# Another warm-up, another order of the first transfers, and new ranks for a planned attention and feed-forward kernel

## Chip, core and metric

The kernel runs on one core of a Trainium2 chip. The metric is the device time of one execution in microseconds, here the median of three runs. Lower is better.

## What is computed

Three parts follow each other: a gated linear attention (4 batches, 8 heads, 768 tokens, head size 32, state size 16), a channel mix with 256 to 1,024 to 256 channels and a sigmoid gate, and a second feed-forward layer with 256 to 2,048 to 256 channels. All of it is computed on 3,072 tokens, in float32.

```python
log_a = np.log(np.clip(a, 1e-06, 1.0))
for c in range(nc):                       # chunks of the sequence
    cum = np.cumsum(la, axis=-1)
    L = np.exp(cum[:, :, :, None] - cum[:, :, None, :]) * causal
    y_intra = (C B^T * L) x
    y_inter = (C state) * exp(cum)
    state = exp(sum(la)) * state + sum(B x * exp(cum[-1] - cum))
xk = mu_k * x + (1 - mu_k) * x_prev;  xr likewise with mu_r
k = relu(xk @ w_k);  v = (k * k) @ w_v;  r = sigmoid(xr @ w_r);  x = r * v
h = x @ w_in;  g = h - tanh(h);  out = g @ w_out
```

## The kernel before

**Tiles.** The tokens are cut into 12 groups of 256 for attention (four chunks of 64) and 6 blocks of 512 for the two feed-forward layers. Every large product is done in three parts (high with high, low weights with high, high with low) on values split into a high and a low half; a block of the channel mix is 4 units, one of the second layer 8 units (`up2`, the polynomial `poly_a` to `poly_c`, `g_high`, `g_low`, `down2`).

**Weights.** They arrive as 64-bit numbers in blocks of 512 KB (`raw`, two buffers), 9 for the channel mix and 16 for the second layer, and each is decoded: `square` on ScalarE, then `top`, `sign`, `bottom`, `guard` on VectorE, `high` on either of the two, `low` on VectorE (lines 322 to 365). `NW` (line 34) says how many of the nine are fetched in the prologue; the others are fetched by the plan when a raw buffer is free. An x block or a bc block of attention has 384 KB.

**Prologue.** `START` (lines 60 to 64) is an order written out by hand; each name is a step in `fns` (lines 711 to 728), and what a step issues on an engine stands in that engine's queue in this order. `qz` clears the tile `quiet`; `wa`, `ws`, `wb` multiply it with itself (`fill`, `small`); their results are not used. `Da`, `Dla`, `Dca` load the decays, `Db0` to `Db2` and `Dx0`, `Dx1` the bc and x blocks, `Dnk` and `Dnr` the two mu vectors, `W` the first weight block or blocks: all are issued by SP, which works in order and waits in order. `cA` to `sD` clip, take logarithms and run sums. `cum` (line 678) splits the running sums and has SP store them to DRAM (`dcum`), from where `pr0` (`prep_rows`, into `kl`) and later `rows` (`sr`, `rr`) read them back. `c0t`, `c1t`, `c0b`, `c1b` spread constant selectors into the right operands of the decays of groups 0 and 1, `x0a` to `x1b` the sums into the same tiles; `h0s` spreads the head selector for `ps`, the scales of batch 0 (line 694), whose exponential is `pe`. `d0`, `d1` are the decays of groups 0 and 1 (line 443), `e0`, `e1` their exponentials (line 458). `dec` and `dexp` (lines 684 to 688) make the factors that `w0` and `w1` (`weigh`, line 462) use; `p0` and `sc1` are scores (line 489), `m0` the mask, `u0` the terms of group 0 (line 514), `h0` its chain of states, `v0` the visit of group 0 (lines 499 to 521), `nu` (line 699) makes 1 - mu from the two mu vectors.

**Plan.** Everything after the prologue is a task with engines, durations, predecessors and a rank. `Plan.run` (line 130) goes through the tasks by its own estimate of time, beginning at `START_AT` per engine: of the tasks that an engine could begin at once, it takes the one of lowest rank, and gives it to that engine. The order that comes out is the order in each engine's queue. `RANK_T` spaces attention's groups, `RANK_F0`, `RANK_F`, `RANK_R`, `RANK_U`, `RANK_D` the channel mix (first block, per block, gate, per unit, downward products), `RANK_W0`, `RANK_W` the nine decodes of its weights, `RANK_E0`, `RANK_E` the first four decodes of the second layer (their tiles exist from the start), `RANK_X0`, `RANK_X` the other twelve, which can begin only when attention's tiles are given back (`reopen`, line 1060), `RANK_G0`, `RANK_G`, `RANK_LAG` the second layer. `SPARE` is added to the rank of a task on VectorE that ScalarE could do as well. `ROOM` and `ENTERED` (line 116) say how many of TensorE's instructions are left in the part of the program that it holds when the plan begins.

Of the kernel before, what the change touches and what calls it, by code (L numbers as in the profile page):

```python
# [16 lines left out]
P = 128  # L17
NB, NH, S, HD, NS = 4, 8, 768, 32, 16
# [8 lines left out]
NC4 = GT // L  # L27
# [3 lines left out]
NP = DFF1 // (2 * P)  # L31
NP2 = DFF2 // (2 * P)

NW = 1
NU2 = NBLK * NP2

NE = 2

SPARE = 14.78
PAUSE = 1.5
RANK_T = 8.22
RANK_F0, RANK_F, RANK_R, RANK_U, RANK_D = 27.22, 21.98, 16.05, 6.75, 13.94
RANK_G0, RANK_G, RANK_LAG = 195.03, 0.0, -2.4
RANK_W0, RANK_W = 6.26, 7.26
RANK_X0, RANK_X = 216.99, -1.01
RANK_E0, RANK_E = 72.19, 13.25

# [6 lines left out]


START = """  # L60
    qz tab Da Dla Dca Db0 Dx0 Db1 Dx1 W Db2 Dnk Dnr seg mk wa ws wb c0t c1t c0b st mk2 tri
    cA lA cC lC sA ss h0s x0a cD lD x0b ps pe d0 e0 dec dexp sD cum c1b s0 x1a x1b p0 w0 m0 ob u0 h0 w1
    still heads r0t r0b spread sc1 d1 e1 v0 pr0 nu
""".split()

START_AT = dict(P=18.0, A=16.6, V=15.5, G=12.0, S=11.5, X=0.0, Y=0.0, Z=0.0)


def t_act(n, more=0.0):
    return 0.172 + n / 1200 + more
# [36 lines left out]
class Plan:  # L109
# [3 lines left out]
    OVERLAP = dict(P=0.0, A=0.09, V=0.08, G=0.04, S=0.0, X=0.0, Y=0.0, Z=0.0)  # L113
    SEEN = dict(P=0.22, A=0.05, V=0.05, G=0.05, S=0.0, X=0.0, Y=0.0, Z=0.0)
    SOON, DMA_ISSUE, DMA_LAND = 0.12, 1.2, 0.9
    ROOM, ENTERED, BLOCK, FETCH, FETCH0, BUSY = 67, 16.6, 256, 3.6, 4.4, 60.0

    def __init__(self):
        self.tasks = []
# [88 lines left out]
def chain_kernel(ctx, tc, xb, a, an, a0, bc, mu_k, mu_r, w_k, w_v, w_r, w_in, w_out, out):  # L208
    nc = tc.nc
    V, A, G, PE = nc.vector, nc.scalar, nc.gpsimd, nc.tensor  # L210
# [15 lines left out]
    def fill(n):  # L226

        for _ in range(n):
            PE.matmul(acc[:, 0], quiet, quiet.unsqueeze(1).to_broadcast([P, NC4, P]), start=True, stop=True)

    def small(n):

        for _ in range(n):
            PE.matmul(acc[0:32, 0, 0:32], quiet[0:32, 0:32], quiet[0:32, 0:32], start=True, stop=True)

    def bank(name, shape=(2, BLK)):
        return pairs.tile([P, *shape], F32, tag="pair", name=name)
# [2 lines left out]
    acc = accp.tile([P, 2, BLK], F32, name="acc")  # L240
# [11 lines left out]
    dec = const.tile([P, NG, NQ, NC4], F32, name="dec")  # L252
    sums = const.tile([P, NU2 + 1], F32, name="sums")
    ones = const.tile([P, 1], F32, name="ones")
    quiet = const.tile([P, P], BF16, name="quiet")
# [124 lines left out]
    CUM, TOK, ROW, NR = 64, 96, 112, 116  # L380
# [54 lines left out]
    pds, early = {}, {}  # L435
# [136 lines left out]
    def prologue(fetch1):  # L572

        t0, t1, t2, t3, t4 = vec("f"), vec("h"), vec("s"), vec("l", F32R), vec("f")
        seg, one = t0[:, 0, 0:GT], t0[:, 1, 0:P]
        la, ca = t4[:, 0, 0:NU], t4[:NC, 1, 0:GT]
        tri, cf = t1[:, 0, 0:P], t3[:NC, :, 0:GT]
        ad, mk = t2[CUM:P, 0, 0:GT], t2[:, 1]
        late, soon, pick = slice(L, L + CQ), slice(L + CQ, L + 2 * CQ), slice(L + 2 * CQ, L + 3 * CQ)
        few = mk[:, 2 * P:2 * P + 2 * NQ]  # L580
        by = [vec("xh").rearrange("p a (b i) -> p (a b) i", i=L) for _ in range(2)]
        held = vec("xl")
        st = early["st"] = held[:, 0, 0:GT].rearrange("p (k h j) -> p k h j", k=2, h=2)
# [4 lines left out]
        def warm(n):  # L588
            return lambda: fill(n)
# [32 lines left out]
        def spread(out, lo, hi, cols, e):  # L622
            n = cols.stop - cols.start
            return lambda: copy(e, out[lo:hi], mk[lo:hi, cols].unsqueeze(2).to_broadcast([hi - lo, n, out.shape[-1]]))

        def causal(out, e):
            return lambda: copy(e, out[0:L], mk[0:L, 0:L].unsqueeze(1).to_broadcast([L, CQ, L]))
# [78 lines left out]
        def rest():  # L706
# [2 lines left out]

        early["fill"] = rest  # L710
        fns = dict(
            qz=lambda: V.memset(quiet, 0.0), wa=warm(2), ws=lambda: small(56), wb=warm(6), wc=warm(2), wd=warm(2), seg=t_seg,
            mk=t_mk, mk2=t_mk2, st=t_st, tri=t_tri, still=t_still, heads=t_heads, spread=t_spread,
            tab=lambda: A.preload_act_table_set("natural_log_exp_and_others"),
            c0t=causal(by[0], "V"), c1t=causal(by[1], "V"), c0b=spread(by[0], CUM, TOK, soon, "A"), c1b=spread(by[1], CUM, TOK, soon, "V"),
            h0s=spread(heads0.rearrange("p k (m n) -> p (k m) n", n=NS), CUM, TOK, pick, "A"),
            r0t=causal(slot(0), "A"), r0b=spread(slot(0), CUM, ROW, late, "A"),
            nu=t_nu,
            Da=load(ad, a0), Dla=load(la, a), Dca=load(ca, an), Dnk=load(mus["k"], mu_k), Dnr=load(mus["r"], mu_r), W=fetch1,
            Db0=lambda: bc_load(0), Db1=lambda: bc_load(1), Db2=lambda: bc_load(2), Dx0=lambda: xb_load(0), Dx1=lambda: xb_load(1),  # L720
            cA=clip(ad), lA=ln(ad), cC=clip(la), lC=ln(la), cD=clip(ca), lD=ln(ca),
            sA=scan(ad, CUM, P), sD=scan(ca, 0, NC), ss=t_sums, x0a=moving(0, 0), x0b=moving(0, 1), x1a=moving(1, 0), x1b=moving(1, 1),
            cum=t_cum, dec=t_dec, dexp=t_dexp,
# [9 lines left out]
    def attention():  # L733

        D, E, MK, CH, GS, BPt, X, XL, BL, PSX, PS = ({} for _ in range(11))
        users = []

        def put(*args, **kw):
            t = add(*args, **kw)
            users.append(t)  # L740
            return t

        def at(k):
            return RANK_T * k

        def scales(b, lo, rank, after):
            take = [(R["pair"], ("pc", b))] + ([(R["er"], b)] if b else [])
            p = put(dict(P=0.62), lambda e: scales_sum(b, lo), after, rank, take, ins=4)
            PSX[b] = put(dict(A=t_act(S - lo)), lambda e: scales_exp(b, lo), [p], rank, uses=[take[0], (R["er"], b)], func="exp")
            return p  # L750

        PS[0] = scales(0, 2 * GT, at(2) - 2, [])
        E[1] = put(dict(Y=16.6), lambda e: None)
        filled = put(dict(A=2 * t_act(1024)), lambda e: early["fill"](), [], at(1))
        first_half, visited = None, put(dict(Z=17.4), lambda e: None)
        for k in range(1, NG + 1):
            if 2 <= k < NG:
                XL[k] = put(dict(S=0.47), lambda e, k=k: xb_load(k), [], at(k - 1.5), [(R["xb"], k)], dma=1.7)
                if k >= 3:
                    BL[k] = put(dict(S=0.47), lambda e, k=k: bc_load(k), [], at(k - 1.8), [(R["bc"], k)], dma=1.7)  # L760
                rw = put(dict(S=0.9), lambda e, k=k: rows(k), [], at(k - 1.2), [(R["rows"], k)], dma=0.2)
                D[k] = put(dict(P=0.7), lambda e, k=k: decays(k), [rw, filled if k == 3 else None], at(k) - 1.5, [(R["pair"], ("pd", k)), (R["L"], k)], [(R["rows"], k)], ins=4)
                E[k] = put(dict(A=t_act(1024)), lambda e, k=k: decays_exp(k), [D[k]], at(k) - 1.5, (), [(R["pair"], ("pd", k)), (R["L"], k)], func="exp")
                BPt[k] = put(dict(V=t_dve(GT)), lambda e, k=k: weigh(k), [XL[k]], at(k) - 1.5, [(R["bp"], k)], [(R["xb"], k)], port=True)
            b, g = divmod(k, NGB)
            if g == 0 and k < NG:
                pr = put(dict(S=0.45), lambda e, b=b: prep_rows(b), [PS.get(b - 2)], at(k - 1.2), (), dma=0.2)
                PS[b] = scales(b, 0, at(k) - 1.7, [pr])
            if k >= 2:
                j = k - 1  # L770
                take = ([(R["pair"], ("pcb", k))] if k < NG else []) + [(R["pair"], ("py", j))]
                use_a = [(R["cp"], j), (R["state"], j), (R["bc"], k)]
                use_b = [(R["pair"], ("py", j)), (R["L"], j), (R["xb"], j), (R["bp"], k), (R["xb"], k)]
                first_half = put(dict(P=(1.7 if j % NGB else 1.6) if k < NG else 0.65), lambda e, j=j: visit_a(j), [CH[j], GS[j], BL.get(k), D.get(k), PS.get(b) if k < NG else None, MK[j]], at(j), take, use_a, ins=192 if k < NG else 128)
                pause = put(dict(X=PAUSE), lambda e: None, [first_half])
                visited = put(dict(P=1.3 if k < NG else 0.8), lambda e, j=j: visit_b(j), [pause, XL.get(j), XL.get(k), BPt.get(k)], at(j), (), use_b, ins=192 if k < NG else 128)
            if k == NG:
                X[j] = put(dict(A=t_act(BLK), V=t_dve(BLK)), lambda e, j=j: group_out(j, e), [visited], at(j), (), [(R["pair"], ("py", j))])
                break
            MK[k] = put(dict(V=t_dve(1024)), lambda e, k=k: mask(k), [first_half, E.get(k)], at(k), (), [(R["pair"], ("pcb", k)), (R["L"], k)])  # L780
            CH[k] = put(
                dict(V=0.32 * moves(k)), lambda e, k=k: chain(k), [visited, PSX[b] if k > 1 else None], at(k) - 0.5,
                ([] if g else [(R["state"], k)]) + ([(R["state"], k + 1)] if g < NGB - 1 else []),
                [(R["pair"], ("py", k - 1)), (R["er"], b)] + ([(R["state"], k)] if g else []), port=True,
            )
            X[k - 1] = put(dict(A=t_act(BLK), V=t_dve(BLK)), lambda e, j=k - 1: group_out(j, e), [CH[k]], at(k - 1), (), [(R["pair"], ("py", k - 1))])
            GS[k] = put(dict(V=t_dve(BLK)), lambda e, k=k: group_scale(k), [BL.get(k), PSX[b] if k > 1 else None], at(k) - 0.5, [(R["cp"], k)], [(R["bc"], k), (R["er"], b)], port=True)
        return X, users
# [358 lines left out]
```

## Time and profile before

| | us |
|---|---|
| median of 3 runs | 499.2 (497.39 to 500.78) |
| the profiled execution, its own time | 499.19 |
| its span, first to last instruction | 497.1 |
| TensorE busy in it | 474.1 (95%) |
| VectorE busy | 402.2 (81%) |
| ScalarE busy | 295.3 (59%) |

In the rows below, PE is TensorE's products, DVE VectorE, ACT ScalarE, POOL GpSimd, SPq the queue of SP that issues transfers. A row of a timeline says when a run of like instructions starts, how long they take together, the line of the kernel, and out<-in by the program's names; in square brackets stands how long the engine had been idle before and what released it. Products are pipelined, so the end of one is modelled and a full engine reads 10.00 of 10 us. PEld is TensorE's loading of weights, which overlaps its products. PEclk, the granted clock, is what the clock's records give as a share of full speed.

### The profile page before, as it was taken

To read this page: it belongs to the slowest core of one execution; us is meant where nothing else is said; L and a number is where in the kernel's file an instruction comes from. 1 tells how busy PE (TensorE), PEld (TensorE's weight loads), DVE (VectorE), ACT (ScalarE), POOL (GpSimd) and SP (SyncE) were. 2 spreads that over 40 slices of the span, in tenths; PEclk is the share of its full clock that TensorE was granted. 3 is DMA by queue.
4 is the path that set the end of the run, shared out by engine and by line. 5 is a ranking of instruction groups with operands and counts; after the bars stand their busy time and mean duration, and the time that the engine had idled before them with its cause. 6 is when DMAs were issued, how large, how long until landed. Compare 5 with 4: busy or idle time off the path is not lost.

```text
span 497.1 us, 9592 instructions
## 1 busy us (share of the span) xinstructions
PE 474.1 (95%) x4121; PEld 378.9 (76%) x4121; DVE 402.2 (81%) x504; ACT 295.3 (59%) x376; POOL 8.9 (2%) x27
## 2 busy tenths in 40 slices
PE   9759899999999999999999999999999999999992
PEld 4437678777778887887788788888878888887882
DVE  7799999999558999997878769767876966788681
ACT  4766886765757776646555654645565365455451
POOL 7000000000000000000000000000000000000000
PEclk9998999999999999999999999999999999999998
DMA  7674453311012312210000100100010010001001
GB/s 238 188 219 157 130 179 107 111 48 33 1 33 98 116 55 85 86 42 1 0 0 1 42 1 0 44 1 0 1 42 1 0 42 2 0 1 42 2 0 48
DMA packets 14120, 27.32 MB, mean 55 GB/s; under 512 B 2256, under 2 KB 3152, under 8 KB 14072
## 3 DMA queue, kind: packets, MB, share of 16 engines
q1 hardware_dynamic: 14072, 26.65, 17.0%
q8 instruction: 34, 0.56, 0.5%
q14 instruction: 14, 0.11, 0.1%
HBM read 23.30 MB, written 3.34 MB: 54 GB/s over the span
## 4 chain that ended last, share of the span: by engine, by line
PE 64%; DVE 22%; ACT 7%; DMA 3%; issue 3%; DVEq 0%; SPq 0%; ACTq 0%
PE acc L806 10%; PE acc L808 9%; PE acc L807 9%; PE ph L796 8%; PE ph L797 8%; PE ph L799 8%; DVE l L829 2%; DVE wd L334 2%; DMA raw<-in_w_k 2%; DVE f L930 2%; DVE wd L337 2%; DVE f L821 2%; PE pk L796 2%; DVE f L934 2%; DVE keep L340 2%
## 5 line engine op out<-in xcount | busy, mean ns | idle before, releaser
L925 ACT ACTIVATE s<-ph 128x1024 f32<-128x1024 f32 (+1 forms) x49 | 49.4, 1009 | 65.1 <-PE ph L799 65.1
L930 DVE SCALAR_TENSOR_TENSOR f<-f,s 128x1024 f32<-128x1024 f32 (+1 forms) x49 | 58.8, 1200 | 30.2 <-ACT f L926 30.1
L369 ACT ACTIVATE h<-f 128x1024 fp32r<-128x1024 f32 (+1 forms) x44 | 45.8, 1041 | 53.2 <-DVE f L934 48.0
L796 PE MATMUL ph<-xh,winh 128*128 128x512 f32 x192 | 74.7, 389 | 0.0
L797 PE MATMUL ph<-xh,winl 128*128 128x512 f32 x192 | 74.7, 389 | 0.0
L806 PE MATMUL acc<-h,wouth 128*128 128x512 f32 x188 | 73.7, 392 | 0.6 <-ACT h L369 0.2
L808 PE MATMUL acc<-l,wouth 128*128 128x512 f32 x188 | 73.4, 391 | 0.7 <-DVE l L943 0.5
L943 DVE TENSOR_TENSOR l<-f,h 128x1024 fp32r<-128x1024 f32 (+1 forms) x49 | 58.9, 1201 | 18.6 <-ACT h L369 18.0
L807 PE MATMUL acc<-h,woutl 128*128 128x512 f32 x188 | 73.2, 389 | 0.0
L934 DVE TENSOR_TENSOR f<-ph,f 128x1024 f32<-128x1024 f32 (+1 forms) x49 | 58.9, 1201 | 3.7 <-DVE f L930 0.5
L799 PE MATMUL ph<-xl,winh 128*128 128x512 f32 x192 | 59.1, 389 | 0.0
L926 ACT ACTIVATE f<-s,biases 128x1024 f32<-128x1024 f32 (+1 forms) x49 | 55.7, 1137 | 1.6
L806 PEld LDWEIGHTS acc<-h,wouth 128*128 128x128 f32 x188 | 35.3, 188 | 9.7 <-ACT f L926 1.5
L808 PEld LDWEIGHTS acc<-l,wouth 128*128 128x128 f32 x188 | 35.3, 188 | 8.9 <-DVE l L943 1.5
L796 PEld LDWEIGHTS ph<-xh,winh 128*128 128x128 f32 x192 | 36.0, 188 | 7.5
L799 PEld LDWEIGHTS ph<-xl,winh 128*128 128x128 f32 x192 | 36.0, 188 | 7.6
L797 PEld LDWEIGHTS ph<-xh,winl 128*128 128x128 f32 x192 | 36.0, 188 | 7.5
L807 PEld LDWEIGHTS acc<-h,woutl 128*128 128x128 f32 x188 | 35.3, 188 | 7.1
L796 PE MATMUL pk<-xh,wkh 128*128 128x512 f32 x96 | 38.9, 405 | 0.1
L806 PE MATMUL acc<-h,wvh 128*128 128x512 f32 x96 | 38.6, 402 | 0.0
L797 PE MATMUL pk<-xh,wkl 128*128 128x512 f32 x96 | 37.8, 394 | 0.0
L807 PE MATMUL acc<-h,wvl 128*128 128x512 f32 x96 | 37.5, 391 | 0.0
(138 smaller groups left out, 748.7 us busy)
## 6 DMA issues: line engine op xcount, KB each, us to landing
bct<-in_bc SPq DMA_DIRECT2D x12, 384.0 KB
xbt<-in_xb SPq DMA_DIRECT2D x12, 384.0 KB
raw<-in_w_in SPq DMA_DIRECT2D x8, 512.0 KB
raw<-in_w_out SPq DMA_DIRECT2D x8, 512.0 KB
out<-ob SPq DMA_DIRECT2D x11, 256.0 KB
raw<-in_w_k SPq DMA_DIRECT2D x4, 512.0 KB
raw<-in_w_v SPq DMA_DIRECT2D x4, 512.0 KB
raw<-in_w_r SPq DMA_DIRECT2D x1, 512.0 KB
```

What stands on the lines that cost most here:

```text
L369: A.activation(out=out, in_=in_, func=AF.Copy)
L796: PE.matmul(o, wh[:, k, ms], hi[:, k], start=k == 0, stop=False)
L797: PE.matmul(o, wl[:, k, ms], hi[:, k], start=False, stop=False)
L799: PE.matmul(o, wh[:, k, ms], lo[:, k], start=False, stop=k == 1)
L806: PE.matmul(acc[:, c], wh[:, k, cs], h[:, e], start=first, stop=False, skip_group_check=True)
L807: PE.matmul(acc[:, c], wl[:, k, cs], h[:, e], start=False, stop=False, skip_group_check=True)
L808: PE.matmul(acc[:, c], wh[:, k, cs], l[:, e], start=False, stop=last, skip_group_check=True)
L925: A.activation(out=s, in_=phs[j, i][:, e], func=AF.Square, accum_out=sums[:, c:c + 1])
L926: A.activation(out=qs[j, i][:, e], in_=s, func=AF.Square, scale=PA, bias=pbias)
L930: V.scalar_tensor_tensor(out=q, in0=q, scalar=PG, in1=s, op0=ALU.add, op1=ALU.mult)
L934: V.tensor_tensor(out=q, in0=phs[j, i][:, e], in1=q, op=ALU.mult)
L943: V.tensor_tensor(out=l[:, e], in0=qs[j, i][:, e], in1=f(h[:, e]), op=ALU.subtract)
```

## The change

The warm-up becomes one row of 48 products of 128 columns (`wa`), in place of two of 512, 56 of 32x32 and six of 512; `small` goes. In `START`, `W` and what stood behind it (`Db2`, `Dnk`, `Dnr`) move behind `cum`, with a second `W` between them, since `NW` is 2: both first blocks of w_k are fetched in the prologue. `c1b` moves from VectorE to ScalarE and ahead of `ps`; `w0` moves ahead of `x1b`. The plan's start times, `ROOM`, `ENTERED` and the ranks get new values, and `filled` the rank of group 2.

```diff
--- before.py
+++ after.py
@@ -31,21 +31,21 @@
 NP = DFF1 // (2 * P)
 NP2 = DFF2 // (2 * P)
 
-NW = 1
+NW = 2
 NU2 = NBLK * NP2
 
 NE = 2
 
 
 
-SPARE = 14.78
+SPARE = 18.29
 PAUSE = 1.5
-RANK_T = 8.22
-RANK_F0, RANK_F, RANK_R, RANK_U, RANK_D = 27.22, 21.98, 16.05, 6.75, 13.94
-RANK_G0, RANK_G, RANK_LAG = 195.03, 0.0, -2.4
-RANK_W0, RANK_W = 6.26, 7.26
-RANK_X0, RANK_X = 216.99, -1.01
-RANK_E0, RANK_E = 72.19, 13.25
+RANK_T = 8.25
+RANK_F0, RANK_F, RANK_R, RANK_U, RANK_D = 27.63, 22.39, 13.84, 6.34, 12.78
+RANK_G0, RANK_G, RANK_LAG = 424.5, 0.0, -6.53
+RANK_W0, RANK_W = 8.36, 6.38
+RANK_X0, RANK_X = 337.01, -1.22
+RANK_E0, RANK_E = 156.89, 4.07
 
 
 
@@ -58,14 +58,14 @@
 
 
 START = """
-    qz tab Da Dla Dca Db0 Dx0 Db1 Dx1 W Db2 Dnk Dnr seg mk wa ws wb c0t c1t c0b st mk2 tri
-    cA lA cC lC sA ss h0s x0a cD lD x0b ps pe d0 e0 dec dexp sD cum c1b s0 x1a x1b p0 w0 m0 ob u0 h0 w1
+    qz tab Da Dla Dca Db0 Dx0 Db1 Dx1 seg mk wa c0t c1t c0b st mk2 tri
+    cA lA cC lC sA ss h0s x0a cD lD x0b c1b ps pe d0 e0 dec dexp sD cum W Db2 W Dnk Dnr s0 x1a w0 x1b p0 m0 ob u0 h0 w1
     still heads r0t r0b spread sc1 d1 e1 v0 pr0 nu
 """.split()
 
 
 
-START_AT = dict(P=18.0, A=16.6, V=15.5, G=12.0, S=11.5, X=0.0, Y=0.0, Z=0.0)
+START_AT = dict(P=15.8, A=14.2, V=13.8, G=12.0, S=12.0, X=0.0, Y=0.0, Z=0.0)
 
 
 def t_act(n, more=0.0):
@@ -113,7 +113,7 @@
     OVERLAP = dict(P=0.0, A=0.09, V=0.08, G=0.04, S=0.0, X=0.0, Y=0.0, Z=0.0)
     SEEN = dict(P=0.22, A=0.05, V=0.05, G=0.05, S=0.0, X=0.0, Y=0.0, Z=0.0)
     SOON, DMA_ISSUE, DMA_LAND = 0.12, 1.2, 0.9
-    ROOM, ENTERED, BLOCK, FETCH, FETCH0, BUSY = 67, 16.6, 256, 3.6, 4.4, 60.0
+    ROOM, ENTERED, BLOCK, FETCH, FETCH0, BUSY = 99, 14.6, 256, 3.6, 4.4, 60.0
 
     def __init__(self):
         self.tasks = []
@@ -226,12 +226,7 @@
     def fill(n):
 
         for _ in range(n):
-            PE.matmul(acc[:, 0], quiet, quiet.unsqueeze(1).to_broadcast([P, NC4, P]), start=True, stop=True)
-
-    def small(n):
-
-        for _ in range(n):
-            PE.matmul(acc[0:32, 0, 0:32], quiet[0:32, 0:32], quiet[0:32, 0:32], start=True, stop=True)
+            PE.matmul(acc[:, 0, 0:P], quiet, quiet, start=True, stop=True)
 
     def bank(name, shape=(2, BLK)):
         return pairs.tile([P, *shape], F32, tag="pair", name=name)
@@ -709,10 +704,10 @@
 
         early["fill"] = rest
         fns = dict(
-            qz=lambda: V.memset(quiet, 0.0), wa=warm(2), ws=lambda: small(56), wb=warm(6), wc=warm(2), wd=warm(2), seg=t_seg,
+            qz=lambda: V.memset(quiet, 0.0), wa=warm(48), wc=warm(2), wd=warm(2), seg=t_seg,
             mk=t_mk, mk2=t_mk2, st=t_st, tri=t_tri, still=t_still, heads=t_heads, spread=t_spread,
             tab=lambda: A.preload_act_table_set("natural_log_exp_and_others"),
-            c0t=causal(by[0], "V"), c1t=causal(by[1], "V"), c0b=spread(by[0], CUM, TOK, soon, "A"), c1b=spread(by[1], CUM, TOK, soon, "V"),
+            c0t=causal(by[0], "V"), c1t=causal(by[1], "V"), c0b=spread(by[0], CUM, TOK, soon, "A"), c1b=spread(by[1], CUM, TOK, soon, "A"),
             h0s=spread(heads0.rearrange("p k (m n) -> p (k m) n", n=NS), CUM, TOK, pick, "A"),
             r0t=causal(slot(0), "A"), r0b=spread(slot(0), CUM, ROW, late, "A"),
             nu=t_nu,
@@ -750,9 +745,9 @@
             return p
 
         PS[0] = scales(0, 2 * GT, at(2) - 2, [])
-        E[1] = put(dict(Y=16.6), lambda e: None)
-        filled = put(dict(A=2 * t_act(1024)), lambda e: early["fill"](), [], at(1))
-        first_half, visited = None, put(dict(Z=17.4), lambda e: None)
+        E[1] = put(dict(Y=14.1), lambda e: None)
+        filled = put(dict(A=2 * t_act(1024)), lambda e: early["fill"](), [], at(2))
+        first_half, visited = None, put(dict(Z=14.8), lambda e: None)
         for k in range(1, NG + 1):
             if 2 <= k < NG:
                 XL[k] = put(dict(S=0.47), lambda e, k=k: xb_load(k), [], at(k - 1.5), [(R["xb"], k)], dma=1.7)
```

## Rows read from the trace of the kernel before

**Rows 1.** Busy us of PE, PEld, DVE, ACT, POOL by stage; PEclk, DMA share, GB/s.

```profile
...
1.10:12.00 10.90, 10.90 (x78) 5.22 (x78) 9.03 (x17) 4.92 (x9) 8.48 (x22) 1.00 0.84 269
12.00:20.00 8.00, 7.21 (x248) 5.02 (x247) 6.32 (x17) 6.10 (x11) 0.00 (x0) 1.00 0.40 112
20.00:40.00 20.00, 11.33 (x447) 8.00 (x449) 17.19 (x35) 14.91 (x22) 0.00 (x0) 0.96 0.80 240
40.00:62.00 22.00, 20.43 (x382) 15.79 (x366) 21.20 (x37) 15.70 (x21) 0.00 (x0) 0.96 0.42 132
62.00:220.00 158.00, 157.20 (x1824) 126.59 (x1823) 142.28 (x206) 109.62 (x133) 0.00 (x0) 1.00 0.25 78
220.00:480.00 260.00, 258.78 (x1134) 211.65 (x1133) 200.07 (x184) 138.24 (x175) 0.00 (x0) 1.00 0.03 11
38.40:41.90 3.50, 3.38 (x76) 2.61 (x68) 3.46 (x7) 1.68 (x3) 0.00 (x0) 0.51 0.21 71
...
```

**Rows 2.** Timeline of VectorE, 0 to 41 us: start, us, line, tiles [idle before <-releaser].

```profile
...
8.22 0.80 DVE L371 COPY xh<-s 32x1024 f32<-32x1024 f32 x1
...
9.86 1.29 DVE L639 TENSOR_TENSOR xh<-s 32x512 f32<-32x512 f32 x2
13.07 0.43 DVE L462 TENSOR_TENSOR bp<-xbt,dec 128x256 f32<-128x256 f32 x1 [1.92 <-ACT dec L688]
...
16.03 0.16 DVE L701 TENSOR_SCALAR omk<-muk 128x2 f32<-128x2 f32 x1
...
24.33 0.43 DVE L331 TENSOR_SCALAR wd<-raw 128x512 uint32<-128x512 uint32 x1 [2.12 <-DMA raw<-in_w_k]
...
38.90 1.22 DVE L829 TENSOR_TENSOR xl<-f,xh 128x1024 fp32r<-128x1024 f32 x1
...
```

**Rows 3.** The chain of waits up to 62 us: start, us, what.

```profile
...
19.47 4.76 DMA raw<-in_w_k
...
```

**Rows 4.** Timeline of TensorE, 1 to 20 us.

```profile
...
1.09 1.04 PE L229 MATMUL acc<-quiet 128*128 128x512 bf16 x2 [1.09 <-DVE quiet L712]
2.06 1.67 PE L234 MATMUL acc<-quiet 32*32 32x32 bf16 x56
3.66 2.74 PE L229 MATMUL acc<-quiet 128*128 128x512 bf16 x6
6.33 2.07 PE L694 MATMUL pc<-xl 32*128 32x256 f32 x4
8.33 3.36 PE L443 MATMUL pd<-xh,xl 128*128 128x512 f32 x4
...
15.17 1.98 PE L443 MATMUL pd<-xh,xl 128*128 128x512 f32 x4
...
19.63 0.70 PE L447 MATMUL pd<-rr,sr 116*128 116x512 f32 x2 [0.29 <-issue]
```

**Rows 5.** Timeline of ScalarE, 0 to 20 us.

```profile
...
2.13 1.05 ACT L369 ACTIVATE xh<-s 32x1024 f32<-32x1024 f32 x1
...
5.60 0.41 ACT L369 ACTIVATE xl<-s 32x256 f32<-32x256 f32 x1 [0.38 <-POOL s L599]
...
8.44 0.60 ACT L697 ACTIVATE er<-pc 128x512 f32<-128x512 f32 x1 [1.99 <-PE pc L694]
11.73 1.08 ACT L458 ACTIVATE L<-pd 128x512 f32<-128x512 f32 x2 [2.69 <-PE pd L443]
...
```

**Rows 6.** Timeline of SP, the engine that issues the transfers, 0 to 24 us.

```profile
...
4.43 0.43 SPq L320 DMA_DIRECT2D raw<-in_w_k  x1
...
7.67 1.78 SPq L682 DMA_DIRECT2D dcum<-l  x2
13.04 0.34 SPq L409 DMA_DIRECT2D kl<-dcum  x1
...
```

**Rows 7.** The instructions of line 331: duration ns min/median/max, first and last start.

```profile
...
L331 DVE TENSOR_SCALAR wd<-raw x25: 419/426/429, 16.2 to 222.7; 128x512 uint32<-128x512 uint32 x25
...
```

**Rows 8.** Groups of VectorE's instructions, 14 to 41 us: busy us, mean ns, idle before.

```profile
...
L334 DVE SCALAR_TENSOR_TENSOR wd<-raw,wd 128x512 uint32<-128x512 uint32 x4 | 2.7, 683 | 0.0
...
```

## The prediction

> **What bounds the kernel now.** Read the busy time by stage first [rows 1]. From 62 to 480 us TensorE is busy for 157.2 of 158 us and 258.8 of 260 us: products follow each other without a hole, and nothing that the change does can take more than about 2 us out of these 418. What can still be won lies before 62 us. From 20 to 40 us TensorE works for 11.3 of 20 us, from 40 to 62 us for 20.4 of 22. VectorE is the busier engine in both (17.2 of 20 and 21.2 of 22). So up to 62 us the kernel goes by VectorE and by what VectorE waits for, and after that by TensorE, which keeps whatever lead it has when it becomes full.
>
> The second view is VectorE's own timeline [rows 2]. The prologue's last step there (`nu`) starts at 16.03 us; the low half `xl` of the first mixed block, after which the first product of the channel mix can start, is made at 38.90 us. Between them the one large wait is the 2.12 us before 24.33 us, for the second block of w_k. The chain of waits [rows 3] goes through the same place: the block is issued at 19.47 us and arrives 4.76 us later. The third view is the prologue on TensorE [rows 4] and ScalarE [rows 5]. Six products of 512 columns take 2.74 us, 1.1 columns per ns: the lower level, 1.2 GHz. The decays of group 0 (`d0`) take 3.36 us at 8.33 us, those of group 1, the same four records of the same shape, 1.98 us at 15.17 us. So TensorE is at the lower level through `d0` and near the higher one (2.4 GHz) at `d1`, although the granted clock reads 1.00 for that stretch [rows 1]; there the products' durations are the better witness. ScalarE waits 1.99 us for `ps` and 2.69 us for `d0`.
>
> **Warm-up.** Removed are 8 products of 512 columns and 56 of 32x32, from 1.09 to 6.40 us, in whose middle there are 1.67 us of small products that use a sixteenth of the array [rows 4]. Put in are 48 products of 128 columns, 6,144 columns: at 1.1 columns per ns 5.5 us, so they end at 6.6 us at the latest, and sooner if the clock rises meanwhile. `ps` needs the selector `h0s`, ready at 6.01 us [rows 5], so the warm-up itself costs 0.2 us at worst. If the dense stretch raises the clock before `ps`, `d0` falls to `d1`'s duration, a saving of 1.38 us, and `ps` (2.07 us) by the same ratio to 1.22 us, 0.85 us: 2.2 us in all. Nothing covers this: `e0` waits for `d0` to its end, `dexp` stands behind `e0` on ScalarE, VectorE then waits 1.92 us for `dexp` before `w0` at 13.07 us [rows 2], and TensorE's `u0` waits for `w0`. So the whole rest of the prologue moves by 2.2 us, `nu` to 13.8 us. Bounds: nothing (the clock does not rise) and 2.2 us. I take the rise: what TensorE did before its first fast stretch was `d0` and its like, full-width products close together, and the new warm-up is such work from 1.09 us on, where the old one broke off for the small ones.
>
> The Trainium skill (TensorE: Matmul & The Clock Gate, Part 1: The HAM clock gate) says that the moment at which the clock is released differs between executions of one kernel. By that rule the kernel before may have risen early in some of its other runs, the median would gain less than this trace suggests, say half of the 1.2 us kept below, and the time would be 496.1 us, inside the forecast's own range. One trace cannot show it.
>
> **The selector copy.** `c1b` leaves VectorE (0.80 us at 8.22 us) for ScalarE, where its twin `c0b` takes 1.05 us. ScalarE is idle from 6.46 to 8.44 us, so it fits before `pe`. The 0.80 us on VectorE are followed by the 1.92 us wait, so they are worth nothing by themselves. Without ScalarE's hole the cost would be 1.05 us on `pe`, which `e0` has cover for until `d0` ends. `w0` ahead of `x1b` on VectorE: its wait for `dexp` now holds `x1b` (half of 1.29 us [rows 2]), for which `d1` waits, but `u0` and `scores(1)` run on TensorE meanwhile. I take zero for both; bounds 0 and 0.7 us lost.
>
> **Transfers.** Before, SP issues `W` at 4.43 us, then the third bc block and the two mu vectors, and the sums at 7.67 us; it can read the sums back (`kl`) only at 13.04 us [rows 6]. Now the sums come first, and since SP works in order, `W`, `Db2`, the second `W`, `Dnk` and `Dnr` all stand behind them: they are issued from 9.45 us on, at about half a microsecond each, to 12.2 us, and `kl` after that, so it gains at most 0.8 us at its issue and then finds 1.44 MB (0.52 + 0.39 + 0.52) ahead of it. At the 269 GB/s of the first stage [rows 1] these take 5.4 us, to 14.8 us. First block of w_k: there at about 12 us, first used after `nu`; covered. Second: about 14.8 us instead of 24.2 us, first used behind the first one's decode of 3.15 us (0.42 [rows 7] + 4 x 0.68 [rows 8]) and a mask; covered. But `nu` reads the mu vectors, which now land last, at about 14.8 us, where VectorE could run it at 13.8 us. So of the 2.2 us VectorE keeps 1.2 us (bounds 0 and 2.2).
>
> **The second block early.** VectorE's 2.12 us wait goes. What is late next are the third and fourth blocks; their buffers come free with the decodes of the first two, so they too start some 3 to 5 us sooner, and from 12 to 20 us the transfers ran at 112 GB/s, so there is room. The first `xl`, ready at 40.1 us now, comes 1.2 + 2.1 = 3.3 us sooner, at 36.8 us. Bounds: 0, if attention's own chain sets that time, and 2.8 us, all of VectorE's idle time from 20 to 40 us.
>
> **The clock's dip.** From 38.4 to 41.9 us the granted clock is 0.51 [rows 1], after a stretch in which TensorE had little to do. TensorE is busy for 3.38 us of it, work that takes 1.7 us less at the high level; half of it lies before the first mixed block is ready and waits for VectorE anyway, which leaves 0.8 us. With a fuller TensorE before, the dip may go: I take half, 0.4 us (bounds 0 and 0.8).
>
> **New ranks and start times.** These only choose which ready task an engine takes. The weights of the second layer are put behind nearly all of the channel mix (E0 from 72 to 157, spaced 4 apart), the remaining ones still ahead of the second layer. All 25 decodes start by 222.7 us [rows 7], two of them per unit of the second layer. VectorE idles 15.7 of the 158 us up to 220 us [rows 1], room for five decodes, so I take zero; bounds: 2 us gained (TensorE's idle time from 62 to 480 us), and the last rival below.
>
> **Sum.** The profiled run took 499.19 us, of which the span is 497.1; the median is 499.2, so no correction is needed. 1.2 + 2.1 + 0.4 = 3.7 us less: **495.5 us**.
>
> **Rivals.**
> *The transfers take the start back.* Sums, mu vectors and the next group's reads stand behind the weights. `kl`, the next x block (0.39 MB) and `sr`, `rr` land near 17 us by the same rate, and `decays(2)`, which ran at 19.63 us [rows 4], could run at 17.4 us: it is a tie. If they come a microsecond later, or `nu` waits to 16 us, the prologue's term is gone: 499.2 - 2.5 = 496.7 us. So would it be if the clock does not rise. For it: before, SP stood from 9.45 to 13.04 us for the sums. Against: the transfers ahead are fewer than those from 20 to 40 us. The Trainium skill (DMA: Bandwidth & Descriptors, Queues, rings and completion order) has each engine consume its descriptors in ring order; by that rule small reads do not overtake weights.
> *The second block early is hidden anyway.* If the first mixed block waits for attention's products and not for VectorE, the 2.1 us go into another wait: 499.2 - 1.6 = 497.6 us. Against: from 20 to 40 us VectorE's 2.8 idle us are 2.1 of this wait, so it hardly rests behind it.
> *More than forecast.* All upper bounds at once: 2.2 + 2.8 + 0.8 = 5.8 us, 493.4 us; with 1 us from the ranks 492.4 us.
> *Slower: decodes slip into the second layer.* There TensorE spends 24 products of 0.228 us (258.8 us over 1,134), 5.5 us, on a unit, while VectorE is busy for 77% [rows 1], 4.2 us. A unit whose two blocks (6.3 us) are decoded meanwhile needs 10.5 us of VectorE, 5 us too much. One such unit undoes the gain (500.5 us); from the second on it is slower: 505.5 us. For it: the last decode starts only at 222.7 us, and E0's four are put off most. Against: the 15.7 us of idle VectorE.
>
> **How the numbers follow.** About 1% is what a measurement of this kernel can tell from no change, 5 us here. Forecast 0.50 (own range 493.7 to 497); transfers or clock 0.19, 496.7; hidden 0.11, 497.6; more 0.14, 492.4; slower 0.06, 505.5. Faster by over 1% (below 494.2 us): the 0.14 and a fifth of the forecast, 0.24. Slower: 0.05. The rest, 0.71, is within 1%. The range from 491.6 us (more, with its spread) to 499.0 us leaves out the slower case and the ends of the others.
>
> **What would show it.** `d0` near 2 us and `e0` near 9.5 us: the warm-up; `d0` at 3.3 us refutes it. `nu` at 14 to 15 us, with or without a wait for the mu vectors: the price of the order. No wait for w_k on VectorE near 22 us; first `xl` ready near 36.8 us instead of 40.1. TensorE's idle time between 20 and 62 us down from 10.2 to about 9 us, its products in `ps` and `d0` shorter by 2. A hole of more than a few microseconds on TensorE between 215 and 250 us would mean the last rival.

## The result and the profile after

| kernel | median us | runs | ratio to before, 95% interval |
|---|---|---|---|
| before | 499.7 | 11 | |
| changed | 494.57 (493.55 to 496.77) | 11 | 0.9912 [0.9894, 0.9930] |

The changed kernel takes 0.9% less, 4.4 us by the ratio. The time is close to the forecast of 495.5 us, but the time was not saved where the forecast put it. The profiled execution took 494.57 us, its span is 492.4 us. Its busy time by stage, with the columns of [rows 1]:

```profile
...
1.10:12.00 10.90, 10.40 (x138) 8.33 (x142) 9.11 (x18) 8.52 (x14) 8.02 (x22) 1.00 0.70 208
12.00:20.00 8.00, 5.20 (x174) 3.35 (x167) 4.75 (x15) 5.34 (x8) 0.00 (x0) 0.95 0.94 305
20.00:40.00 20.00, 16.60 (x471) 12.14 (x471) 19.36 (x38) 13.42 (x20) 0.00 (x0) 0.67 0.64 196
40.00:62.00 22.00, 22.00 (x438) 17.19 (x436) 21.04 (x36) 18.64 (x24) 0.00 (x0) 0.93 0.49 149
62.00:220.00 158.00, 157.67 (x1738) 127.04 (x1738) 145.15 (x212) 108.02 (x128) 0.00 (x0) 1.00 0.25 76
220.00:480.00 260.00, 259.36 (x1139) 212.88 (x1138) 198.20 (x182) 140.72 (x181) 0.00 (x0) 1.00 0.03 11
...
```

Compared with [rows 1], TensorE works for 16.6 instead of 11.3 us from 20 to 40 us and for all of the 22 us after it. From 62 to 480 us it is idle for 1.0 us instead of 2.0. But from 20 to 40 us its granted clock is 0.67, a good part of that stretch at the lower level (1.2 GHz), where it had been 0.96; so part of the busy time is the same work done more slowly.

The prologue on TensorE, to be held against [rows 4]:

```profile
...
1.09 4.99 PE L229 MATMUL acc<-quiet 128*128 128x128 bf16 x48 [1.09 <-DVE quiet L707]
6.07 1.12 PE L689 MATMUL pc<-xl 32*128 32x256 f32 x4
7.12 1.99 PE L438 MATMUL pd<-xh,xl 128*128 128x512 f32 x4
...
13.08 1.96 PE L438 MATMUL pd<-xh,xl 128*128 128x512 f32 x4 [0.43 <-DVE st L558]
...
17.90 0.35 PE L416 MATMUL pc<-kl,heads 16*128 16x256 f32 x1 [0.98 <-DMA kl<-dcum]
19.64 0.77 PE L442 MATMUL pd<-rr,sr 116*128 116x512 f32 x1 [1.39 <-DVE L L544]
```

`ps` takes 1.12 us instead of 2.07, `d0` 1.99 instead of 3.36: 2.3 us. The rise of the clock came as forecast, during or right after the warm-up. `d1` begins 2.1 us sooner. The decays of group 2 begin at 19.64 us, no sooner than in the kernel before (19.63 us). Then VectorE, beside [rows 2]:

```profile
...
10.48 0.43 DVE L457 TENSOR_TENSOR bp<-xbt,dec 128x256 f32<-128x256 f32 x1 [0.67 <-ACT dec L683]
...
17.46 0.17 DVE L696 TENSOR_SCALAR omk<-muk 128x2 f32<-128x2 f32 x1 [3.11 <-DMA muk<-in_mu_k]
...
20.60 0.42 DVE L326 TENSOR_SCALAR wd<-raw 128x512 uint32<-128x512 uint32 x1
...
37.04 1.22 DVE L824 TENSOR_TENSOR xl<-f,xh 128x1024 fp32r<-128x1024 f32 x1
...
```

`w0` comes 2.6 us sooner than at 13.07, but `nu` is 1.4 us later than at 16.03: VectorE stood 3.11 us for the mu vectors. The first decode of w_k starts only at 20.60 us, the first `xl` at 37.04 instead of 38.90 us, 1.9 us sooner where the forecast had 3.3. No wait for w_k is left on VectorE. SP's issues and the transfers' rate in single microseconds (the last two columns are the share of the 16 DMA engines and GB/s) show why:

```profile
...
7.66 1.80 SPq L677 DMA_DIRECT2D dcum<-l  x2
9.51 0.51 SPq L315 DMA_DIRECT2D raw<-in_w_k  x1
...
10.57 0.44 SPq L315 DMA_DIRECT2D raw<-in_w_k  x1
11.05 0.47 SPq L587 DMA_DIRECT2D muk<-in_mu_k  x1
...
12.41 1.23 SPq L404 DMA_DIRECT2D kl<-dcum  x1
...
```

```profile
...
9.00:10.00 1.00, 1.00 (x27) 0.78 (x29) 0.79 (x2) 0.86 (x2) 0.80 (x4) 1.00 0.45 132
...
11.00:12.00 1.00, 1.00 (x48) 0.91 (x52) 0.99 (x2) 0.99 (x2) 0.00 (x0) 1.00 0.92 193
12.00:13.00 1.00, 0.65 (x24) 0.41 (x16) 1.00 (x3) 0.90 (x2) 0.00 (x0) 1.00 0.90 241
...
14.00:15.00 1.00, 1.00 (x9) 0.23 (x9) 0.34 (x2) 0.00 (x0) 0.00 (x0) 1.00 1.04 408
...
```

The order of the issues is the forecast's, and so are their times, to within 0.2 us. The rate begins lower, 132 to 241 GB/s from 9 to 13 us, while the stores of the sums (which the forecast left out) and the first packets of `W` are under way, and is higher later. Over the eight microseconds up to the arrival of mu it is this:

```profile
9.50:17.50 8.00, 6.49 (x244) 4.45 (x242) 4.07 (x11) 5.36 (x10) 0.68 (x3) 1.00 0.88 270
```

That is the rate of the forecast, 269 GB/s. But 8 us at 270 GB/s are 2.2 MB, where the forecast counted 1.44 MB: the stores are 0.2 MB, and the other 0.5 MB fit the reads issued behind mu (`kl`, an x block, `sr`, `rr`), by an estimate from their sizes.

How far TensorE is ahead at a given time can be worked out from its records: give each product the distance at which such products follow each other when TensorE is full and the clock is at the higher level (0.23 us for 512 columns), add up what is still to do, and look up when the kernel before had as much left. A kernel that works at half the clock loses lead. These are figures of one execution each, and they shift by up to 0.3 us with the distances taken for the smallest products. This is their table in us:

| at (time in before) | changed | new warm-up alone | new ranks alone | changed, mu first | changed, one block | changed, old ranks |
|---|---|---|---|---|---|---|
| 20 | -0.3 | 1.6 | -0.4 | 0.8 | 1.0 | -2.0 |
| 40 | 2.4 | 0.5 | -0.3 | 3.6 | 3.7 | 0.1 |
| 45 | 0.7 | 0.7 | -0.5 | 4.2 | 4.4 | -0.9 |
| 62 | 2.8 | 1.1 | 1.1 | 4.7 | 5.6 | -0.8 |
| 100 | 2.7 | 1.1 | 1.2 | 4.7 | 1.8 | -1.7 |
| 140 | 3.2 | 1.1 | 1.4 | 5.2 | 2.3 | -1.6 |
| 240 | 4.2 | 1.4 | 2.0 | 6.2 | 2.9 | -1.1 |

The changed kernel has 2.8 of its 4.6 us (the spans are 497.08 and 492.45 us) when TensorE becomes full, and the rest comes after that, where the forecast expected nothing.

### The profile page after: what moved, and what is told of

Read it like the earlier page. It is cut to its first block, busy times and chain, and to the rows that moved or that the text cites. A ratio compares the mean times of both kernels' runs of the same rounds, so it can differ in the third digit from the quotient of the medians.

```text
span 492.4 us, 9561 instructions
## 1 busy us (share of the span) xinstructions
PE 475.2 (96%) x4105; PEld 384.0 (78%) x4105; DVE 400.4 (81%) x505; ACT 296.6 (60%) x375; POOL 8.4 (2%) x27
## 4 chain that ended last, share of the span: by engine, by line
PE 70%; DVE 18%; ACT 3%; DMA 3%; issue 3%; POOL 1%; SPq 0%; POOLq 0%; DVEq 0%; ACTq 0%
PE acc L801 10%; PE acc L803 10%; PE acc L802 10%; PE ph L794 8%; PE ph L791 8%; PE ph L792 8%; PE pk L791 3%; PE pk L792 3%; PE pk L794 3%; PE pcb L484 2%; DVE wd L332 2%; DVE f L925 2%; DVE l L824 2%; PE py L494 2%; DVE f L929 2%
```

## Experiments

Theory A: the prologue's gain is real and is lost to the wait for mu; the second block is worth about 2 us. Its rivals: the warm-up carries everything, or the waits only move. As neither explained the size of the gain, the ranks were tried next. Times are medians; ratios are to runs of the kernel before on the same chip.

**1. The mu transfers first** (on the changed kernel)

```diff
-    qz tab Da Dla Dca Db0 Dx0 Db1 Dx1 seg mk wa c0t c1t c0b st mk2 tri
+    qz tab Da Dla Dca Db0 Dx0 Db1 Dx1 Dnk Dnr seg mk wa c0t c1t c0b st mk2 tri
-    ... cum W Db2 W Dnk Dnr s0 ...
+    ... cum W Db2 W s0 ...
```

> The changed kernel with the two small mu transfers issued ahead of the sums, into the gap that SP has before them; nothing else moves. Theory A (the faster prologue is lost because VectorE stands 3.1 us before `nu` for mu, which lands behind 1.4 MB of weights): `nu` at about 14.4 us without a wait, first `xl` 1.5 to 3 us sooner than 37.0 us, 492 to 493.5 us. Rival B (the read-back of the sums or the second weight block would hold VectorE to the same moment): `nu` early, but the mask and the decode behind it wait instead, 494 to 495 us.

494.03 us, ratio 0.9910 [0.9891, 0.9929]: by the medians the same as the changed kernel. On VectorE, and among what TensorE waited for from 14 to 222 us:

```profile
...
14.26 0.16 DVE L696 TENSOR_SCALAR omk<-muk 128x2 f32<-128x2 f32 x1
...
16.18 1.23 DVE L544 TENSOR_TENSOR L<-pcb,L 128x1024 f32<-128x1024 f32 x1 [1.08 <-ACT L L453]
...
21.02 0.69 DVE L428 TENSOR_TENSOR cp<-bct,er 128x512 f32<-128x512 f32 x1 [1.21 <-ACT er L419]
...
36.18 1.22 DVE L824 TENSOR_TENSOR xl<-f,xh 128x1024 fp32r<-128x1024 f32 x1
...
```

```profile
...
PE pd L442 <- DMA sr<-dcum: 0.8, 1, 0.8
PE pc L416 <- DMA kl<-dcum: 0.8, 1, 0.8
...
```

The wait for mu is gone and `nu` is 3.2 us sooner, but 1.08 us of it go into a wait for `e1` and 1.21 us into one for the scales of the next groups (their products waited 0.8 us for `kl`, but experiment 11 shows that this is not what holds them); the first `xl` is 0.9 us sooner. So rival B holds: behind the mu vectors other waits stand almost as late. (The one profiled execution, 492.9 us, is the fastest of its six, and its large lead in the table is that execution's; 0.1 us by the ratios is all that is measured.)

**2. The old warm-up in the changed kernel**

```diff
-            PE.matmul(acc[:, 0, 0:P], quiet, quiet, start=True, stop=True)
+            PE.matmul(acc[:, 0], quiet, quiet.unsqueeze(1).to_broadcast([P, NC4, P]), start=True, stop=True)
-wa=warm(48)
+wa=warm(2), ws=lambda: small(56), wb=warm(6)
```

> The changed kernel with the old warm-up (8 products of 512 columns and 56 small ones). Theory A: `d0` takes 3.4 us again and ends 2.2 us later, but VectorE waits for mu until 17.5 us as before, so the time stays at 494.6 us, within 0.7. Rival C (the warm-up is what gives the gain): 496.5 to 497.5 us.

494.98 us, 0.9920 [0.9900, 0.9941], within half a microsecond of the changed kernel. But the reason given was only half right. TensorE in this execution:

```profile
...
6.33 1.46 PE L694 MATMUL pc<-xl 32*128 32x256 f32 x4
7.72 1.98 PE L443 MATMUL pd<-xh,xl 128*128 128x512 f32 x4
...
```

`d0` takes 1.98 us here, with the old warm-up: the clock rose before it. The warm-up and `ps` are the same instructions in all six profiled kernels with the old warm-up, and this is the only one of them in which that happened; in the other five `d0` takes 3.36 to 3.78 us. In the eight with the new one it takes 1.98 or 1.99 us every time. So this run does not show what a late clock would have cost here.

**3. The new warm-up alone in the kernel before** (the same edit the other way round)

> The kernel before with the new warm-up alone; the mu transfers are early there. Theory A: `d0` near 2 us, `nu` at 13.8 us instead of 16.0, and the lead is kept in full where nothing late stands in its way, about 497.5 us, or 1 to 2.2 us under before. Rival D (the wait for the second weight block, issued only behind attention's x block, takes it back): `nu` early, VectorE's wait at 24 us longer by the same 2 us, time as before within 0.5 us.

497.81 us, 0.9977 [0.9966, 0.9987]: 1.1 us. VectorE:

```profile
...
14.19 0.16 DVE L701 TENSOR_SCALAR omk<-muk 128x2 f32<-128x2 f32 x1
...
23.83 0.43 DVE L331 TENSOR_SCALAR wd<-raw 128x512 uint32<-128x512 uint32 x1 [3.45 <-DMA raw<-in_w_k]
...
38.01 1.22 DVE L829 TENSOR_TENSOR xl<-f,xh 128x1024 fp32r<-128x1024 f32 x1
...
```

Here the mu vectors are early and `nu` is 1.84 us sooner, as expected. Then the wait for the second block of w_k is 3.45 instead of 2.12 us, and the first `xl` is 0.9 us sooner. Theory A and rival D each hold in part: of the 1.84 us, 1.33 are taken back at that wait.

**4. Two blocks alone in the kernel before**

```diff
-NW = 1
+NW = 2
-    ... Dx1 W Db2 Dnk Dnr seg ...
+    ... Dx1 W Db2 Dnk Dnr W seg ...
```

> The kernel before with both first blocks of w_k fetched in the prologue (NW of 2, the second `W` behind the mu transfers and ahead of the sums), old warm-up, old ranks. Theory A: VectorE's 2.1 us wait for w_k goes, first `xl` 2 to 3 us sooner, 1.5 to 2.5 us under before. Rival E (hidden anyway): the wait moves to another transfer or product, within 0.7 us of before.

498.83 us, 0.9991 [0.9976, 1.0006]: nothing that can be told from zero. VectorE:

```profile
...
23.85 0.69 DVE L346 TENSOR_TENSOR wkl<-keep,wkh 128x512 fp32r<-128x512 f32 x1 [0.62 <-ACT wkh L369]
...
30.04 0.69 DVE L346 TENSOR_TENSOR wkl<-keep,wkh 128x512 fp32r<-128x512 f32 x1 [1.62 <-ACT wkh L369]
...
39.29 1.22 DVE L829 TENSOR_TENSOR xl<-f,xh 128x1024 fp32r<-128x1024 f32 x1
...
```

VectorE no longer waits for w_k's transfer, and then waits 0.62 and 1.62 us for ScalarE's `high` of the very same blocks. The first `xl` comes at 39.29 us, 0.4 us later than before; as much was lost ahead of it, since `d0` took 3.78 us in this execution and `nu` came 0.45 us later (16.48 us). The wait moved (rival E).

**5. One block in the changed kernel**

```diff
-NW = 2
+NW = 1
-    ... cum W Db2 W Dnk Dnr s0 ...
+    ... cum W Db2 Dnk Dnr s0 ...
```

> The changed kernel with NW of 1: the second `W` goes, the plan fetches that block when it can, and the mu vectors land about 1.7 us sooner. New warm-up and new ranks stay. Theory J (the second block early is worth 2 to 3 us): 496.5 to 497.5 us, VectorE waits for w_k near 22 us. Theory K (what it gives, the mu vectors behind it cost): 494 to 495 us.

496.82 us, 0.9950 [0.9933, 0.9967]: the second block early is worth 1.9 us there, close to what theory J said, and by another way. VectorE does not wait for w_k, and the first `xl` comes at 36.07 us, 1.0 us sooner than in the changed kernel: without the second `W` ahead of them the mu vectors land 1.0 us sooner (`nu` at 16.48 us). The loss comes later:

```profile
...
20.00:40.00 20.00, 14.46 (x484) 10.78 (x477) 19.75 (x38) 13.17 (x20) 0.00 (x0) 0.91 0.66 217
...
62.00:100.00 38.00, 35.81 (x492) 27.88 (x489) 36.44 (x59) 27.86 (x34) 0.00 (x0) 1.00 0.38 125
...
```

The changed kernel in the last of these stretches:

```profile
62.00:100.00 38.00, 38.00 (x571) 30.30 (x574) 37.34 (x59) 30.84 (x37) 0.00 (x0) 1.00 0.41 125
```

From 62 to 100 us TensorE works for 35.8 of 38 us, in several waits of 0.3 to 0.6 us for VectorE and ScalarE, where the changed kernel has none; in the table the lead falls from 5.6 to 1.8 us there.

**6. The new ranks alone in the kernel before** (SPARE, all RANK lines, `filled` at `at(2)`)

> The kernel before with the new ranks alone (SPARE, all RANK values, the rank of `filled`); prologue, START_AT and NW as before. So far the new warm-up alone gave about 1.2 us and the two blocks alone about 0.4, while all together gave 4.4 to 5. Theory G (the rest, some 3 us, comes from the ranks by themselves): 495.5 to 497 us. Theory H (the ranks pay only together with the early block and the start times they were chosen for): within 1 us of before. The kernel's author-independent rival I (ranks hold TensorE up at the second layer): over 500 us.

495.89 us, 0.9938 [0.9915, 0.9960]: 3.1 us, two thirds of what the whole change gives. What TensorE waited for between 40 and 220 us, in the kernel before and in this one:

```profile
...
PE py L499 <- ACT L L458: 2.0, 2, 1.3
...
```

```profile
...
PE acc L806 <- issue: 0.3, 1, 0.3
...
PE py L499 <- ACT L L458: 0.2, 1, 0.2
```

The kernel before waited twice for ScalarE's exponential of the decays, 1.3 us at 53 us and 0.7 us at 135 us. Both are gone but for 0.2 us.

**7. The old ranks in the changed kernel**

> The changed kernel with the old ranks; new prologue, start times and NW. Theory G: the 3 us are lost, 497 to 498.5 us. Theory H: worse than each part alone suggests, 498 us or more, with holes on TensorE after 62 us. Theory J (prologue and second block carry the gain): 494 to 495.5 us.

501.44 us, 1.0046 [1.0027, 1.0065]: slower than before, and 6.7 us (0.0134 of 499) slower than the changed kernel. Prologue, transfers, second block and the new start times of the plan together lose 2.3 us under the old ranks. TensorE from 20 to 62 us:

```profile
...
PE pd L442 <- ACT er L419: 3.2, 1, 3.2
PE pd L442 <- ACT xall L364: 3.0, 1, 3.0
PE pk L791 <- ACT L L453: 1.7, 1, 1.7
...
```

Three waits for ScalarE of 7.9 us together. The longest one of the changed kernel in that stretch:

```profile
PE pd L442 <- ACT er L419: 2.3, 1, 2.3
...
```

It waits 0.6 and 0.5 us for ScalarE beside that. The kinds are the same (exponentials and copies on ScalarE); when their turn comes is what the ranks decide.

**8. The ranks of attention and channel mix alone** (SPARE, T, F, R, U, D, W, `filled`; kernel before) **and 9. those of the second layer alone** (G, LAG, X, E; kernel before)

> The kernel before with only those new ranks that order attention, the channel mix and the nine decodes of its weights (SPARE, RANK_T, F0, F, R, U, D, W0, W and the rank of `filled`). All new ranks together gave 3.1 us on it. Theory P (the gain is made before 62 us, where TensorE waited 1.3 us for ScalarE's exponential at 53 us): 2 to 3 us under before, no such wait near 53 us. Theory Q (the gain lies in the second layer's decodes): within 0.7 us of before.

> The kernel before with only the new ranks of the second layer and its decodes (G0, LAG, X0, X, E0, E). Theory P: 0.3 to 1 us under before, made between 130 and 240 us, where all new ranks together took 0.8 us of TensorE's idle time away. Theory Q: 2 to 3 us under before. The forecast's last rival (decodes slip into the second layer): 500 us or more, a hole on TensorE near 220 to 250 us.

The first: 499.02 us, 1.0002 [0.9981, 1.0024]. The second: 498.50 us, 0.9981 [0.9963, 0.9999], 0.9 us. Together (experiment 6) they gave 3.1. The trace of the first shows where its gain went. It has no wait for that exponential near 53 us. Reckoned as in the table above it is 1.3 us ahead at 62 us and 1.2 us at 470 us; in the last two units TensorE then waits:

```profile
...
PE acc L808 <- DVE l L943: 1.6, 1, 1.6
PE acc L806 <- DVE h L371: 0.7, 1, 0.7
```

The kernel before has neither wait; there the low half of the last unit but one is made before the polynomial of the last (in its turn this kernel does not have a wait of 1.4 us that the kernel before has behind these units, for the last sums on VectorE). With both sets of new ranks (experiment 6) the lead of 470 us is still there at the end, so the early ranks' gain reaches the end only with the late ones. The second kernel loses the 0.7 us wait at 135 us and keeps the one at 53; it is level with the kernel before at 62 us (0.1 us behind) and 0.9 us ahead at 240 us. The two leads add up to that of experiment 6, 2.0 us at 240 us. Neither shows a hole of more than 1 us on TensorE near 220 to 250 us.

**10. The old ranks of the second layer in the changed kernel**

> The changed kernel with the old ranks of the second layer and its decodes, the other new ranks kept. With all old ranks it took 501.4 us. Theory P: 495 to 496 us. Theory Q: 499 us or more.

495.88 us, 0.9927 [0.9902, 0.9952]: 0.7 us more than the changed kernel by the ratios, whose intervals overlap; theory P. By difference that would leave 6 of the 6.7 us of experiment 7 to the early ranks, if the parts add up there; the old early ranks alone were not tried in the changed kernel.

**11. The mu transfers first and the second `W` behind `pr0`**

```diff
-    ... cum W Db2 W s0 ... v0 pr0 nu
+    ... cum W Db2 s0 ... v0 pr0 W nu
```

> The changed kernel with the mu transfers ahead of the sums and the second `W` behind the read-back of the sums (`pr0`), so that `kl` finds 0.9 instead of 1.4 MB ahead of it. With the mu vectors first alone VectorE's lead at `nu` (3.2 us) shrank to 0.9 us at the first `xl`, since TensorE then waited for `kl` and `sr` and ScalarE for TensorE. Theory N (the small reads behind the weights hold attention there): `kl` lands 1.5 us sooner, first `xl` 1 to 2 us sooner than 36.2 us, 492.5 to 493.5 us. Rival: the second block, later now, makes VectorE wait as before, 494 to 495 us.

495.01 us, 0.9918 [0.9896, 0.9939]. TensorE's wait for `kl` is gone, the first `xl` comes at 36.37 us and nothing is gained: a miss. The small reads behind the weights are not what holds attention there. ScalarE's own queue is, in experiment 1 (shown first) as here:

```profile
17.43 0.66 ACT L322 ACTIVATE keep<-raw 128x512 f32<-128x512 f32 x1 [0.54 <-DMA raw<-in_w_k]
...
20.61 0.38 ACT L419 ACTIVATE er<-pc 128x256 f32<-128x256 f32 x1
...
```

```profile
17.61 0.66 ACT L322 ACTIVATE keep<-raw 128x512 f32<-128x512 f32 x1 [0.57 <-DMA raw<-in_w_k]
...
20.80 0.38 ACT L419 ACTIVATE er<-pc 128x256 f32<-128x256 f32 x1
...
```

In both it waits for the second weight block to make its `square`, copies constants for 2.1 us, and only then makes the scales, 3.2 us later, without a pause. So in both the scales stand behind what the plan put ahead of them on ScalarE, a wait of half a microsecond for the second block among it. (`sr` came no sooner here, but the decays that need it end at 19.8 us, before ScalarE comes to them at 21.07 us.)

**12. The clock held up** (on experiment 1)

```diff
+    def hold(n):
+        for _ in range(n):
+            PE.matmul(acc[:, 0], quiet, quiet.unsqueeze(1).to_broadcast([P, NC4, P]), start=True, stop=True)
+        if 1 <= k <= 2:
+            hold(4)                # at the end of visit_b
-    ... v0 pr0 nu
+    ... v0 wc pr0 nu               # wc is hold(6)
```

> The changed kernel with the mu transfers first, and 14 idle products of 512 columns (6 behind the visit of group 0, 4 behind each of the visits of groups 1 and 2), meant to keep the granted clock up from 19 to 40 us, where it is 0.5 for 10 to 17 us. They cost TensorE about 3 us of stretches in which it mostly waits. Theory L (the dips cost 1 to 2 us of the path): no record at 0.5 before 60 us, 492 to 493 us. Rival M (TensorE waits for VectorE there anyway): the clock is held and the time is that of the kernel with the mu vectors first, 494 us, or up to 1 us longer.

494.24 us, 0.9897 [0.9873, 0.9921]. Without and with the extra products:

```profile
...
20.00:40.00 20.00, 17.00 (x484) 12.81 (x488) 18.34 (x34) 13.45 (x21) 0.00 (x0) 0.76 0.63 192
...
```

```profile
...
20.00:40.00 20.00, 17.00 (x482) 11.93 (x482) 17.42 (x33) 13.88 (x21) 0.00 (x0) 0.83 0.61 194
...
```

The clock is 0.83 instead of 0.76 from 20 to 40 us; the dip got shorter and did not go. The time is the same. That agrees with rival M, but as some two thirds of the dip are still there, what a full clock would give stays open.

## Why the prediction was right, and where it was not

**Warm-up: right in mechanism and size, wrong in what it is worth.** 2.2 us were forecast for `ps` and `d0`, 2.3 were measured. Alone it gives 1.1 us. Taken out of the change it costs 0.4 us, not distinguishable from nothing; but in the one traced execution of that run the clock rose early all the same. The rule of the Trainium skill that was weighed against it (TensorE: Matmul & The Clock Gate, Part 1: The HAM clock gate: the moment of the release differs between executions) agrees with the traces, as far as executions of kernels that are alike up to `d0` can show it: with the old warm-up the clock rose before `d0` in one of six executions and later in five. What the new one bought is that it was early in all eight.

**Selector copy: right.** `c1b` fits into ScalarE's hole (6.48 to 7.53 us) and `pe` starts right behind it, at 7.55 us.

**Transfers: the term that was mis-sized.** The forecast saw that mu would land behind the weights and put it at 14.8 us, with 1.2 us of the prologue's gain kept. It came at 17.4 us, and `nu` was 1.4 us later than before. Mis-sized is what moves before mu is there, 2.2 MB instead of 1.44, and not the rate, 270 GB/s for the 269 of the forecast: the stores of the sums were left out, and reads issued behind mu. The bytes ahead are not all of it, since with 0.52 MB less of them (experiment 5) mu came 1.0 us sooner, where 269 GB/s would give 1.9. So the condition of the first rival was met (`nu` past 16 us, the decays of group 2 no sooner than before), and the time was still not its 496.7 us. The price of the mistake is small, since experiment 1 shows that behind mu VectorE would have waited for ScalarE.

**Second block: right in amount, wrong in place.** Inside the change it is worth 1.9 us (forecast 2.1), by itself nothing. The forecast's path, VectorE's wait goes and the first `xl` moves up, does not hold: in experiment 4 the wait turned into others, and in experiment 5 the first `xl` was even sooner without the block, since mu landed sooner. What it saves are TensorE's waits between 62 and 100 us, as far as one execution shows.

**The dip: wrong in sign.** 0.4 us less were forecast; instead the low clock lasted longer (0.67 from 20 to 40 us). In the table it costs the changed kernel 1.7 us of lead between 40 and 45 us, all of which is back at 62 us; in the kernel before TensorE waited 1.3 us in between.

**Ranks: the step that failed.** "I take zero" was the wrong value for what turned out to be the largest term: 3.1 us alone, 6.7 us within the change. The bound of 2 us was taken from TensorE's idle time after 62 us, as if ranks acted only there. The late ones do, with 0.9 us (experiment 9). The early ones act before 62 us (1.3 us ahead there in experiment 8), where TensorE's waits for ScalarE depend on which task the plan puts first. The last rival, decodes slipping into the second layer, did not come: TensorE is full from 220 us on.

**Sum.** The effects do not add in both directions: put into the kernel before, -1.1 (warm-up), -0.4 (two blocks, not distinguishable from nothing) and -3.1 (ranks) come near the whole, but the same parts taken out of the change are worth 0.4, 1.9 and 6.7 us. New ranks without the new prologue gain; the new prologue with the old ranks loses. The total was met by luck: a term that was too large (3.3 us for prologue and block) and one that was too small (none for the ranks) made up for each other. Why a given set of ranks suits one prologue and not the other was seen only as the waits above, in one execution each; it is not settled further than that. The plan's new start times and the new order of the transfers were never tried alone, so what they take or give is open.

No version tried is distinguishable from the changed kernel on the better side: experiments 1 and 12 have the lowest ratios, 0.9910 and 0.9897, within its interval.

## What to carry to other kernels

When an order of work is planned from start times and priorities, new priorities are a change of their own: cost them in the stretch where engines still wait for each other, and test them apart from the rest. When a load is moved behind others, look for the smallest transfer that moves with it and for the instruction that needs it; here two vectors of 1 KB held VectorE for 3.1 us. And before a wait is counted as a gain, look for what stands second in the same place: three of the waits removed here came back as others (experiments 1, 4 and 11).

## What the runs showed of the hardware

In the kernel before, after a microsecond without any transfer (19 to 20 us), the transfers ran at 203 and in the next microsecond at 363 GB/s. In the changed kernel, with the stores of the sums ahead of the weights, it took longer: 132 GB/s from 9 to 10 us, 193 from 11 to 12, 408 from 14 to 15; what part of that is the stores' was not tested. With the old warm-up the rise of TensorE's clock came before or after the same product in different executions (`d0` of 1.98 or of 3.36 to 3.78 us). And the low clock from 20 to 40 us, where TensorE waits for others much of the time, could be shortened (granted clock 0.83 instead of 0.76) without a change of the time that could be measured (494.24 and 494.03 us).
